# The second expert's output by seven products in two of three token groups instead of one

## The chip, the cores and the metric

The kernel runs on one core of a Trainium2 chip. The metric is the device time of one launch in microseconds (us). Three runs of the kernel before took 972.09, 972.25 and 973.09 us, with a median of 972.25. The engines of the core are TensorE (PE, with its weight loads PEld), VectorE (DVE), ScalarE (ACT), GpSimd (POOL) and SyncE (SP), which issues nearly all DMA transfers here.

## The reference, cut to what matters

```python
attn = block_causal_attention(q, k, v)       # 4 batches x 8 heads, 576 tokens, head size 64
x = attn.reshape(2304, 512)
y = (silu(x @ w_gate) * (x @ w_val)) @ moe_w_out      # first expert, 1536 wide
h = y @ w_in                                          # second expert, 2048 wide
out = where(h > 0, h, exp(min(h, 0)) - 1) @ w_out     # 2304 x 512
```

## The kernel before

**Arithmetic.** Every fp32 product is three matmuls on rounded parts: with a = hi + lo for each operand, hi·hi, lo·hi and hi·lo (`mm3`, L212 to L215, and the output products L1113 to L1115 and L1222 to L1224, which have the same form). "Splitting" an operand means writing its hi with ACT and its lo = operand − hi with DVE or POOL.

**Seven products.** A 2x2 block product needs eight block products. The scheme used here gets by with seven, named M1 to M7, and pays with sums of blocks of both operands before the product (the operands' "sums"), splits of these sums, and adds of the results ("keep" copies a PSUM bank to SBUF, "plus" adds a bank to it). It is used in the gate and value products of some chunks (`sg_unit`, L1374; the sums of its weights lie in the DRAM tile g_scr), for the output of the first expert (`y_group`, L744), for h of the second expert (`p3_h`, L1015) and, in one group of tokens, for its output (`p3_o7`, L1138).

**Stages.** Attention and the first expert's gate stage come first and overlap. Then the tokens run in three groups of 768, each two halves of 384. `y_group` makes y in three groups one after another (466 to 594 us of the profiled execution, the y stage). Then for each group 0, 1 and 2: y is read back and split (`p3_y`, L836; sums L852, hi L860, lo L861), h is made in eight pairs p of 256 columns of W_in (42 matmuls of 384 columns each), the elu is applied and the output product taken. With the constant S7 = 2 (L47), groups 0 and 1 take the plain output product `p3_o` (36 matmuls of 512 columns for each pair, 288 in a group, laid between the h products of the next pair; `p3_drain`, L1121, copies the six banks out). Group 2 takes `p3_o7` behind all its h: 7 products x 8 pairs x 3 blocks of 128 tokens x 3 matmuls = 504 matmuls of 256 columns. Its operand sums are 32 DVE operations (L1149), its 56 splits are an ACT copy (L1157) and a lo (L1158) on POOL where the product is M1 or the pair is 3 or 7, on DVE else; the drains are L1177 (ACT) and L1186 (DVE).

**Weights.** Inputs arrive as 64-bit words; `conv_unit` (L293) loads a block into "raw", DVE makes fp32 of it in a tile c (L196 to L200), ACT writes hi, and DVE or POOL lo. All of W_out ends as the resident parts OH (tiles oh) and OL (ol). The seven-product output needs five kinds of sums or copies of W_out for each pair: `o_sums` (L923) makes them during group 1: it adds OH + OL back to fp32 (L934, 16 DVE operations), takes 32 sums (L940), splits them (hi L950 on ACT, lo L951 on POOL) and stores them in the DRAM tiles o_scr; `o_slot` (L966) loads them from there. The weights of h are loaded from w_scr in the same way, into slots of xa and other tiles.

**Order.** A planner (class Plan, L61 to L147) takes each operation with an engine, a cost, a due time and what it reads and writes, simulates the engines, and writes one fixed program for each engine. Engines then wait for each other only through data and buffers. The loop at the end of the program (L1520 on) hands the steps of the second expert to the planner in the order i, p.

## Time and profile before

| | us |
|---|---|
| median of three runs | 972.25 |
| the profiled execution | 971.81 |
| its span | 970.0 |
| PE busy | 961.0 (99%) |
| DVE busy | 792.4 (82%) |
| ACT busy | 647.0 (67%) |
| POOL busy | 209.3 (22%) |

The profiled execution took 971.81 us, 0.44 us less than the median; 1.81 us of it lie around the span. PE is busy nearly all of the span, so time is won or lost where PE does less or waits. The stages by PE's work are: attention and gate stage up to 466 us, the y stage to 594, group 0 to 732, group 1 to about 846 with the first h of group 2 behind it, and group 2's output by seven products from 904 to 967.

### The profile page before, as it was taken

What the parts mean: (1) busy time and instruction counts of PE and PEld (TensorE: products, weight loads), DVE (VectorE), ACT (ScalarE), POOL (GpSimd) and SP (SyncE); (2) the same over time, 40 slices, a digit from 0 to 9 for tenths busy, and PEclk for the clock granted to TensorE, in tenths of its full rate; (3) what the DMA queues carried; (4) which work ended last, traced back from release to release, by engine and by line L of the source; (5) the groups of instructions that cost most, each with busy time, mean ns of one, the idle gap of its engine ahead of it and who ended that gap; (6) DMA issues with size and microseconds to landing.
All of it is one profiled execution on the core that took longest, in us unless ns stands there. A gap on an engine that the chain in (4) does not pass through costs nothing.

```text
span 970.0 us, 18622 instructions
## 1 busy us (share of the span) xinstructions
PE 961.0 (99%) x6266; PEld 872.7 (90%) x6266; DVE 792.4 (82%) x1637; ACT 647.0 (67%) x1521; POOL 209.3 (22%) x220
## 2 busy tenths in 40 slices
PE   9999999999999999999999999999999999999998
PEld 8789988888888978888999999988899999999998
DVE  6989677767776796699999996989988887868993
ACT  6998578878988644456766675666665555666643
POOL 3334442233315623000000200020001222111231
PEclk9999999999999999999999999999999999999999
DMA  6756465666586669866762802788747676678663
GB/s 226 233 193 219 137 204 163 214 189 218 169 260 209 231 234 336 273 221 199 248 198 88 292 35 83 233 256 303 227 131 217 205 262 206 183 255 256 218 213 115
DMA packets 116463, 202.56 MB, mean 209 GB/s; under 512 B 12304, under 2 KB 51216, under 8 KB 116368
## 3 DMA queue, kind: packets, MB, share of 16 engines
q1 hardware_dynamic: 116224, 201.24, 63.8%
q8 instruction: 50, 0.82, 0.3%
q14 instruction: 45, 0.37, 0.1%
q10 hardware_dynamic: 144, 0.13, 0.0%
HBM read 141.56 MB, written 59.77 MB: 208 GB/s over the span
## 4 chain that ended last, share of the span: by engine, by line
PE 93%; DVE 3%; ACT 2%; issue 1%; DMA 0%; POOL 0%; SPq 0%; ACTq 0%
PE gv L213 7%; PE gv L215 7%; PE gv L214 7%; PE y L213 6%; PE y L214 6%; PE y L215 6%; PE tp L509 5%; PE h L213 5%; PE h L215 5%; PE h L214 5%; PE sa L483 4%; PE o L1115 4%; PE o L1113 4%; PE o L1114 4%; PE tp L604 2%; PE o L1222 2%
## 5 line engine op out<-in xcount | busy, mean ns | idle before, releaser
L213 PE MATMUL gv<-xa,bt 128*128 128x256 f32 x240 | 72.7, 303 | 0.6 <-DVE tt L658 0.6
L213 PE MATMUL gv<-xa,val 128*128 128x256 f32 x240 | 71.9, 300 | 0.0
L609 ACT COPY th<-tp 128x512 f32<-128x512 f32 x96 | 53.5, 590 | 22.1 <-PE tp L605 21.7
L215 PE MATMUL gv<-xa,val 128*128 128x256 f32 x240 | 67.1, 280 | 0.5 <-POOL val L210 0.5
L214 PE MATMUL gv<-xa,bt 128*128 128x256 f32 x240 | 67.0, 279 | 0.0
L215 PE MATMUL gv<-xa,bt 128*128 128x256 f32 x240 | 67.0, 279 | 0.0
L214 PE MATMUL gv<-xa,val 128*128 128x256 f32 x240 | 67.0, 279 | 0.0
L213 PE MATMUL h<-val,xa 128*128 128x384 f32 x194 | 65.2, 336 | 0.0
L215 PE MATMUL h<-val,xa 128*128 128x384 f32 x194 | 65.1, 336 | 0.0
L214 PE MATMUL h<-val,xa 128*128 128x384 f32 x194 | 65.1, 336 | 0.0
L764 ACT ACTIVATE val<-a 128x384 fp32r<-128x384 f32 x80 | 41.3, 525 | 28.3 <-PE y L215 26.6
L1324 POOL TENSOR_TENSOR wy<-c,wy 128x256 fp32r<-128x256 f32 x48 | 39.3, 831 | 88.2 <-ACT wy L1323 88.1
L509 PE MATMUL tp<-th,rv 128*64 128x256 f32 (+1 forms) x512 | 55.5, 359 | 0.0
L918 POOL TENSOR_TENSOR val<-c,val 128x256 fp32r<-128x256 f32 x14 | 12.0, 863 | 196.4 <-ACT val L917 196.4
L918 POOL TENSOR_TENSOR wy<-c,wy 128x256 fp32r<-128x256 f32 x42 | 32.5, 786 | 86.6 <-ACT wy L917 65.6
L951 POOL TENSOR_TENSOR a<-c,a 128x256 fp32r<-128x256 f32 x22 | 19.4, 888 | 146.2 <-ACT a L950 146.2
L653 DVE SCALAR_TENSOR_TENSOR tt<-tt,gv 128x256 f32<-128x256 f32 x60 | 25.0, 416 | 31.4 <-ACT tt L649 31.1
L509 PEld LDWEIGHTS tp<-th,rv 128*64 128x64 f32 x512 | 33.9, 136 | 18.2 <-ACT c L188 0.3
L483 PE MATMUL sa<-rk,rq 64*128 64x320 f32 (+2 forms) x192 | 49.9, 393 | 0.0
L483 PE MATMUL sb<-rk,rq 64*128 64x320 f32 (+2 forms) x192 | 49.9, 393 | 0.0
L213 PEld LDWEIGHTS gv<-xa,bt 128*128 128x128 f32 x240 | 45.3, 189 | 4.8 <-issue 2.6
L213 PEld LDWEIGHTS gv<-xa,val 128*128 128x128 f32 x240 | 45.3, 189 | 2.3 <-issue 2.3
(431 smaller groups left out, 3655.3 us busy)
## 6 DMA issues: line engine op xcount, KB each, us to landing
xa<-w_scr SPq DMA_DIRECT2D x168, 256.0 KB, 3.1
a<-a_scr SPq DMA_DIRECT2D x67, 192.0 KB, 3.4
g_scr<-wy SPq DMA_DIRECT2D x48, 256.0 KB, 2.9
xa<-g_scr SPq DMA_DIRECT2D x48, 256.0 KB, 4.2
w_scr<-wy SPq DMA_DIRECT2D x42, 256.0 KB, 4.0
xa<-o_scr SPq DMA_DIRECT2D x40, 256.0 KB, 3.1
raw<-in_w2i_dram SPq DMA_DIRECT2D x16, 512.0 KB, 4.6
raw<-in_w2o_dram SPq DMA_DIRECT2D x16, 512.0 KB, 4.0
```

The lines of the kernel that those rows point to most:

```text
L213: pe.matmul(dst, wh, xh, start=start, stop=False, skip_group_check=more)
L214: pe.matmul(dst, wh, xl, start=False, stop=False, skip_group_check=more)
L215: pe.matmul(dst, wl, xh, start=False, stop=stop, skip_group_check=more)
L483: pe.matmul(sc[2 * p + j][:, at:at + w], raw["rq"][us, QW * p + 128 * q:QW * p + 128 * q + 128], raw["rk"][us, ext * p + o:ext * p + o + w ...
L509: pe.matmul(st["pv"][64 * j:64 * j + 64, QW * p + o:QW * p + QW], raw["rv"][:, p * (nf + 1) + c, 64 * j:64 * j + 64], x[:, at:at + QW - o] ...
L609: act.copy(out["th", c // 2], st["tr", c])
L764: add("ACT", 412, lambda: act.activation(t(0), ab(p, r, g), ACTF.Copy, scale=0.5), by(u, p), [abk(p, r)], [hk], ([("xcd", o, 0) for o in ( ...
L918: add("POOL", 1000, lambda: pool.tensor_tensor(t()[:, 256:512], part(*x), t()[:, 0:256].bitcast(F32), ALU.subtract), prio, [ck(*x), hk] + ...
L1113: pe.matmul(d, h, OH[f][:, cs], start=(p == 0 and u < 2), stop=False, skip_group_check=True)
L1114: pe.matmul(d, h, OL[f][:, cs], start=False, stop=False, skip_group_check=True)
L1115: pe.matmul(d, l, OH[f][:, cs], start=False, stop=(p == HP - 1 and u > 1), skip_group_check=True)
L1324: add("POOL", 800, lambda: pool.tensor_tensor(t()[:, 256:512], part(*x), t()[:, 0:256].bitcast(F32), ALU.subtract), prio, [ck(*x), hk] + w ...
```

## The change

- S7 is 1: group 1 takes `p3_o7` too, and only group 0 the plain output product.
- The fp32 form of each block of W_out is stored in new DRAM tiles wf_scr once it is converted (`keep_whole`), and `o_sums` loads it from there instead of adding OH + OL; its lo parts go from POOL to DVE. `o_sums` runs for pairs 0 to 4 in group 0 and for 5 and 6 in group 1 (`steps`); pair 7 is converted in the y stage (`early`) and its sums made there (`y_sums`).
- In `y_group` the signs of the weights' sums are turned so that some operand sums become adds in place, and these become DMAs issued by POOL that add the source into the destination (`accum`): one of the two sums before M5 in every group, and both before M6 in group 1 (GA). They take the place of 30 of 72 DVE sums.
- `sg_unit` gives the first two units of the gate stage buffers of their own for the results that are kept, so the planner can lay the products of the two units between each other.
- Buffers move: raw is one tile, one tile of the elu's results lies in it, and four of the six drains of group 0 go to pa_t.

```diff
-S7, HSTEP, OSTEP, OLEAD, PLO, GC, OSL = 2, 7.35, 8.47, 8.0, (3, 7), 1, 6.0
+S7, HSTEP, OSTEP, OLEAD, PLO, GC, OSL = 1, 7.35, 8.47, 8.0, (3, 7), 1, 6.0
+    wf_scr = [dram.tile([128, DM], F32, name=f"wf_scr{f}") for f in range(K2)]
...
+    def keep_whole(f, prio):
+        i = unit["o", f]
+        add("SP", 450, lambda: sp.dma_start(out=wf_scr[f], in_=cv_state[i][1]), prio, [("c", cn[i], 0), ("c", cn[i], 1)], [("wf", f, 0)], data=728)
+
+    def early(f, prio):
+        conv_unit(unit["o", f], prio, whole=True, first=[("w", 2 * K1 - 1 - x, 0) for x in range(3)])
+        keep_whole(f, prio - 1)
...
+        def accum(p, d, x, u):
+            add("POOL", 1000, lambda: pool.dma_start(out=ab(p, d, g), in_=ab(p, x, g), accum_op=ALU.add), by(u, p) - 4, [abk(p, x), abk(p, d)], [abk(p, d)], data=HT * 2.84)
...
             if o == M6:
                 for p in range(KP):
-                    comb(p, 1, 3, 1, ALU.subtract, u)
-                    comb(p, 0, 1, 0, ALU.add, u)
+                    if g != GA:
+                        comb(p, 1, 3, 1, ALU.add, u)
+                        comb(p, 0, 1, 0, ALU.add, u)
+                    else:
+                        accum(p, 1, 3, u)
+                        accum(p, 0, 1, u)
             if o == M5:
                 for p in range(KP):
-                    comb(p, 2, 2, 0, ALU.subtract, u)
-                    comb(p, 0, 3, 0, ALU.subtract, u)
+                    accum(p, 2, 0, u)
+                    comb(p, 0, 0, 3, ALU.subtract, u)
...
+    def o_sums(p, prio, after=[]):
...
+            def load(c=c):
+                full[c] = conv.tile([128, 512], F32, tag="c", name="c", bufs=4)
+                sp.dma_start(out=full[c], in_=wf_scr[2 * p + c])
...
-            add("POOL", 740, lambda: pool.tensor_tensor(t()[:, 256:512].bitcast(F32R), part(*x), t()[:, 0:256], ALU.subtract), prio, [ck(*x), hk], [lk], data=-3000)
+            add("DVE", 420, lambda: dve.tensor_tensor(t()[:, 256:512].bitcast(F32R), part(*x), t()[:, 0:256], ALU.subtract), prio, [ck(*x), hk], [lk], data=-1000)
...
+    seq = "i6 i7 o0 o1 o2 o3 o4 s0 o5 s1 o6 s2 s3 s4 o7".split()
...
-            if i == S7 - 1:
-                o_sums(p, due3[i, p] + OSL)
+            if i == S7 and p == 0:
+                for x in (5,6,):
+                    o_sums(x, due3[i, 0] + 6 * (x - 5) + 2)
```

On PE in the gate stage of seven products, at the first unit's M7 (a bank gv, weights in xa): before, the last product of M7 is followed by M4 into the same bank.

```order
L213 MATMUL gv<-val_132,xa 128x512
L214 MATMUL gv<-val_453,xa 128x512
L215 MATMUL gv<-val_132,xa 128x512
L213 MATMUL gv<-val_132 128x512
L214 MATMUL gv<-val_132 128x512
L215 MATMUL gv<-val_132 128x512
```

The same place after:

```order
L215 MATMUL gv<-val_147,xa 128x512
L216 MATMUL gv<-val_468,xa 128x512
L217 MATMUL gv<-val_147,xa 128x512
L215 MATMUL y_4756<-val_147,xa 128x512
L216 MATMUL y_4756<-val_468,xa 128x512
L217 MATMUL y_4756<-val_147,xa 128x512
L215 MATMUL y_4756<-val_147,xa 128x512
L216 MATMUL y_4756<-val_468,xa 128x512
L217 MATMUL y_4756<-val_147,xa 128x512
L215 MATMUL gv<-val_147 128x512
L216 MATMUL gv<-val_147 128x512
L217 MATMUL gv<-val_147 128x512
```

Six matmuls of the second unit's M7, into a bank y, now stand between the first unit's M7 and its M4.

On POOL from the last weights of the first expert's output into the y stage, before (wy and val hold split weights):

```order
L1324 TENSOR_TENSOR wy_98<-c,wy_98 128x256 x6
L918 TENSOR_TENSOR wy_98<-c,wy_98 128x256 x14
L918 TENSOR_TENSOR val_453<-c,val_453 128x256 x7
L210 TENSOR_TENSOR bt_106<-c,bt_105 128x512
L918 TENSOR_TENSOR val_453<-c,val_453 128x256 x7
```

And after (a and a_N are the operand blocks of the first expert's output):

```order
L982 TENSOR_TENSOR wy_114<-c,wy_114 128x256 x14
L816 DMA a<-a 128x384 x2
L816 DMA a_5974<-a 128x384
L816 DMA a_5975<-a 128x384
L816 DMA a_5976<-a 128x384
L816 DMA a_5977<-a 128x384
L816 DMA a_5984<-a_5978 128x384
L816 DMA a_5985<-a_5979 128x384
L816 DMA a_5986<-a_5980 128x384
L816 DMA a_5987<-a_5981 128x384
L816 DMA a_5988<-a_5982 128x384
L816 DMA a_5989<-a_5983 128x384
```

The first six are the sums before M5 of the first group, the next six the first of two rows of sums before M6 of the second group; six more of the second row (each adds what the first row made) and twelve before M5 of the second and third group follow.

On DVE in the output by seven products, around the sums of M5, before (group 2; L1149 sums, L1158 lo parts, L1186 drains):

```order
L1149 TENSOR_TENSOR a<-a 128x384
L1158 TENSOR_TENSOR bt_122<-g_9615,bt_121 128x384
L1158 TENSOR_TENSOR bt_124<-g_9619,bt_123 128x384
L1186 TENSOR_TENSOR xq_140<-o_7317,xq_140 128x512
L1186 TENSOR_TENSOR xq_140<-o_7318,xq_140 128x256
L1149 TENSOR_TENSOR a<-a 128x384 x2
L1149 TENSOR_TENSOR raw_100<-raw_100,ar_144 128x384
L1158 TENSOR_TENSOR bt_126<-a,bt_125 128x384
```

And after, in group 1, behind the sums of M5 (L1243 lo parts, L1271 drains, L916 and L925 the sums and lo parts of the next group's y):

```order
L1243 TENSOR_TENSOR val_147<-g_8637,val_147 128x384
L916 TENSOR_TENSOR xq_157<-yq_5970,yq_5969 128x768
L925 TENSOR_TENSOR wy_114<-yq_5969,wy_114 128x768
L1243 TENSOR_TENSOR bt_137<-g_8645,bt_136 128x384
L916 TENSOR_TENSOR xq_158<-tt,xq_157 128x768
L1271 TENSOR_TENSOR xq_155<-o_7398,xq_155 128x512
L1271 TENSOR_TENSOR xq_156<-o_7399,xq_156 128x256
L1243 TENSOR_TENSOR bt_139<-tt,bt_138 128x384
L1243 TENSOR_TENSOR bt_141<-a,bt_140 128x384
L1243 TENSOR_TENSOR val_147<-ar_159,val_147 128x384
L925 TENSOR_TENSOR wy_114<-xq_157,wy_114 128x768
```

The sums and splits of y for group 2 (ten operations of 768 columns in all) stand between the lo parts of group 1's seven products; before, they stood beside the plain output products.

## Rows read from the trace of the kernel before

**Rows 1.** The page's chain that ended last, shares of the span by engine.

```profile
PE 93%; DVE 3%; ACT 2%; issue 1%; DMA 0%; POOL 0%; SPq 0%; ACTq 0%
```

**Rows 2.** Windows: PE, PEld, DVE, ACT, POOL busy (instructions), PEclk, DMA share, GB/s.

```profile
466.00:594.00 128.00, 128.00 (x734) 127.45 (x735) 124.79 (x250) 84.63 (x170) 6.48 (x7) 1.00 0.49 158
594.00:732.00 138.00, 137.93 (x702) 125.43 (x701) 116.58 (x215) 86.38 (x183) 6.84 (x8) 1.00 0.70 224
...
856.00:904.00 48.00, 48.00 (x278) 47.91 (x277) 39.84 (x70) 33.55 (x79) 7.27 (x7) 1.00 0.83 258
904.00:967.00 63.00, 62.90 (x525) 62.60 (x523) 48.91 (x89) 31.16 (x67) 18.69 (x13) 1.00 0.56 183
```

**Rows 3.** Timeline of PE: start, duration in us, engine, line, operation, out<-in.

```profile
512.46 0.34 PE L213 MATMUL y<-val,wy 128*128 128x384 f32 x1
...
587.42 0.34 PE L213 MATMUL y<-val,bt 128*128 128x384 f32 x1
...
732.05 0.39 PE L1113 MATMUL o<-xa,val 128*128 128x512 f32 x1
...
856.12 0.40 PE L1115 MATMUL o<-oh,bt 128*128 128x512 f32 x1
...
904.20 0.33 PE L1222 MATMUL o<-xa,val 128*128 128x256 f32 x1
...
966.62 0.28 PE L1224 MATMUL o<-bt,bt 128*128 128x256 f32 x1
```

**Rows 4.** All waits of PE's weight loads from 600 us on: total, count, longest.

```profile
PEld h L213 <- DVE xq L1067: 0.5, 1, 0.5
PEld h L213 <- ACT xq L1071: 0.3, 1, 0.3
```

**Rows 5.** Timeline of PE and SP's queue, start of the seven-product gate stage; brackets: idle before.

```profile
351.76 1.47 SPq L1371 DMA_DIRECT2D xa<-g_scr  x3
...
354.76 0.39 PE L215 MATMUL gv<-xc,bt 128*128 128x512 f32 x1
355.30 0.50 PE L213 MATMUL gv<-xc,bt 128*128 128x512 f32 x1 [0.15 <-DVE tt L658]
...
361.14 0.39 PE L215 MATMUL gv<-val,xa 128*128 128x512 f32 x1
362.21 0.50 PE L213 MATMUL gv<-val 128*128 128x512 f32 x1 [0.68 <-ACT xq L1391]
```

**Rows 6.** Tile g_scr, 330 to 372 us: time from issue to landing of its transfers.

```profile
DMA to landing us min/median/max: 2.0/4.1/6.9
```

**Rows 7.** Timeline of SP's queue and PE in the y stage, second group.

```profile
506.06 3.59 SPq L749 DMA_DIRECT2D a<-a_scr  x4
...
524.96 0.34 PE L213 MATMUL y<-val 128*128 128x384 f32 x1
```

**Rows 8.** Tile a_scr, 480 to 520 us: time from issue to landing of its transfers.

```profile
DMA to landing us min/median/max: 2.3/3.0/3.9
```

**Rows 9.** Timeline of DVE, PE and POOL in group 2's output by seven products.

```profile
913.70 0.55 DVE L1158 TENSOR_TENSOR val<-g,val 128x384 fp32r<-128x384 f32 x1
...
917.15 0.28 PE L1224 MATMUL o<-bt,val 128*128 128x256 f32 x1
...
928.77 2.99 POOL L1158 TENSOR_TENSOR bt<-a,bt 128x384 fp32r<-128x384 f32 x1 [6.73 <-PE o L1224]
...
931.99 0.28 PE L1224 MATMUL o<-xa,bt 128*128 128x256 f32 x1
...
937.78 1.13 POOL L1158 TENSOR_TENSOR val<-g,val 128x384 fp32r<-128x384 f32 x1 [2.50 <-ACT val L1157]
```

**Rows 10.** Groups by line on DVE: count, busy us, mean ns of one, idle before.

```profile
L940 DVE TENSOR_TENSOR c<-c 128x256 f32<-128x256 f32 x32 | 14.1, 447 | 1.5 <-POOL a L951 1.2
L861 DVE TENSOR_TENSOR val<-tt,val 128x768 fp32r<-128x768 f32 x6 | 5.7, 952 | 0.1
```

More of the change, by code (lines that the diff above doesn't have):

```diff
@@ L95, in add @@
         deps.discard(i)
-        self.tasks.append((eng, ns, fn, prio, deps, data, order - deps - {i}, {"POOL": "DVE", "DVE": both and "POOL"}.get(eng), whole))
+        self.tasks.append((eng, ns, fn, prio, deps, data, order - deps - {i}, {"POOL": data <= 0 and "DVE", "DVE": both and "POOL"}.get(eng), whole))
     def order(self):
@@ L776, in keep @@
         def keep(r, m):
-            add("ACT", 450, lambda: act.copy(dst(r, m), bank(X, m)), PMP, [bk(X, m)], [dk(r, m)], free)
+            add("ACT", 450, lambda: act.activation(dst(r, m), bank(X, m), ACTF.Copy, scale=-1.0 if r % 2 else 1.0), PMP, [bk(X, m)], [dk(r, m)], free)
         def plus(r, m, b):
@@ L1515, in attention_moe_moe_kernel, with steps @@
         y_group(g, due2[g])
-    for m, p in W2SEQ[PRE0 + KP:]:
-        if m == "o" and p == 0:
-            add("NONE", 0, to_p3, PT0, writes=[("p3", 0, 0)], behind="p2")
-        if m == "i":
-            p3_weights(p, due3[0, p] - 50, True)
-        else:
-            for f in (2 * p + 1, 2 * p):
-                conv_unit(unit["o", f], due3[0, p] - 20, after=[w2_free(f)])
+    for n, e in enumerate(sorted(EARLY)):
+        early(e, due2[1] + 4 + 4 * n)
+        if e % 2:
+            i = unit["o", e - 1]
+            y_sums(e // 2, due2[1] + 4 + 4 * n + 1, i)
+    add("NONE", 0, to_p3, PT0, writes=[("p3", 0, 0)], behind="p2")
+    def steps(seq):
+        for x in seq:
+            m, p = x[0], int(x[1:])
+            if m == "i":
+                p3_weights(p, due3[0, p] - 50, True)
+            elif m == "s":
+                o_sums(p, due3[0, p] + 20)
+            else:
+                for f in (2 * p + 1, 2 * p):
+                    late(f, due3[0, p] - 20, [w2_free(f)])
+    seq = "i6 i7 o0 o1 o2 o3 o4 s0 o5 s1 o6 s2 s3 s4 o7".split()
+    first = next(n for n, x in enumerate(seq) if x[0] == "s")
+    steps(seq[:first])
     last = None
```

134 lines of the change are left out of this document (96 added, 38 removed).

## The prediction

> **What bounds the kernel now.** I read the chain that ended last first: 93% of it is PE, 3% DVE [rows 1]. The windows by stage come next. From 466 to 967 us PE is busy to within 0.2 us in every stage [rows 2], and from 600 us on its weight loads waited twice, 0.5 and 0.3 us [rows 4]. So there the time is the number of matmuls times their pitch. A single matmul's row shows 0.28 to 0.40 us, but matmuls overlap, and what counts is the distance between starts. With no wait between, two starts and the count of matmuls give it [rows 3]:
> 384 columns, 432 matmuls of the y stage: (587.42 − 512.46) / 432 = 0.1735 us.
> 512 columns: from 732.05 to 856.12 stand all 288 output products of group 1 and 336 of 384 columns, so (124.07 − 336 × 0.1735) / 288 = 0.2284 us.
> 256 columns: from 904.20 to 966.62 stand the 504 of group 2 with 18 h products among them, so (62.42 − 18 × 0.1735) / 503 = 0.1179 us.
>
> The granted clock is 1.00 in all stages [rows 2] and PE stays as busy, so I take that level (2.4 GHz) and these pitches for the new program. What can spoil them is an operand that is late. DVE is the engine to watch: 124.79 of 128 us in the y stage, 116.58 of 138 in group 0, 39.84 of 48 in group 2's h, 48.91 of 63 in its seven products [rows 2]. At 97% in the y stage it still delays nobody, so a high share alone costs nothing; a short lead does.
>
> **Part 1, the swap on PE.** Group 1 loses 288 matmuls of 512 columns and gets 504 of 256: 504 × 0.1179 − 288 × 0.2284 = 59.42 − 65.78 = **−6.4 us**. It lies wholly on the path. Seven products save an eighth of the columns, 12.5%; here 9.7%, because the short matmul costs a little more per column.
>
> **Part 2, the gate stage.** Before, three gaps stand at the start of the seven-product units. The one that the new order can fill: M7's last matmul starts at 361.14, the next at 362.21, with ACT's copy of the bank (L1391) between [rows 5]. At 0.23 us a matmul that is a gap of 0.84. Six matmuls of the second unit, 1.4 us of work, now stand there. Against it the second unit's weights are wanted earlier: their loads are issued at 351.76 and land after a median of 4.1 us [rows 5, 6], at 355.9, and the second unit's first product is now wanted at about 355.0. That is −0.8 to +0.9, and with two smaller gaps (355.30 less 354.76 is 0.54, so 0.31 [rows 5]) −1.5 to +0.9. The planner can lay other products first, so I take **−0.6**.
>
> **Part 3, the accumulating DMAs.** They remove 30 DVE sums and 30 waits of a kind that no row shows: no DMA of the kernel before is issued by POOL. The nearest rows for what one costs POOL are its own operations on 384 columns, 1.13 us alone and 2.99 beside DVE [rows 9]; for the landing, 2.3 to 3.9 us of SP's loads of the same blocks [rows 8]. Call the first c, the second L. The tight place is the second group's two rows of sums before M6. Their last operand is loaded by the last of four transfers issued from 506.06 to 509.65 [rows 7]; issued at about 509.3, it lands 3.0 later, at 512.3. Behind that POOL issues the sixth sum of the first row and six of the second: ready at 512.3 + 7c + L. M6 starts at 524.96 [rows 7] and comes to its third pair of blocks after 24 matmuls, at 529.1; less a hi and a lo of 0.55 each [rows 9] that is 528.0. The spare is 15.7 us. With c = 1.13 and L = 3.0 the chain takes 10.9: hidden. With c = 2 and L = 3.9 it takes 17.9: 2.2 us lost. With c = 2.99 and L = 3.9 it takes 24.8: 9.1 lost. I take **0**, by the 1.13, since POOL has only 6.48 us of other work in that stage [rows 2]. The sums before M5 come two products later and have more room. What the 30 sums free on DVE is used by the conversion of pair 7, which moves into that stage, so DVE is as busy there as before.
>
> The page "SBUF — State Buffer" of the Trainium skill, section "Who interferes with whom", says that DVE's copies and tensor_scalar operations in a two-port mode lock GpSimd out of the port with which it writes descriptors, so that a DMA it issues is starved, while DVE's two-input operations hold only GpSimd's reads. By that the y stage's DVE program, nearly all two-input operations, would leave c near its undisturbed value, and the few conversions of pair 7 would stretch single issues. No trace of before shows a POOL-issued DMA. By the Trainium skill's page "DMA: Bandwidth & Descriptors", section "Anatomy of one DMA — SWDGE (gpsimd) path", 2.0 us and 196.6 KB at 436 KB per us give an estimate of 2.45 us for L; the sum by it would be the same.
>
> **Part 4, group 0.** DVE gets the sums and lo parts for five pairs, 40 operations at 0.447 = 17.9 [rows 10], and loses the conversion of two blocks, which I leave out: at most 116.58 + 17.9 = 134.5 of 138, 97%. The y stage runs at 97% without a wait, so this is hidden; its cover is that these sums are needed only in group 1. SP moves more there: 20 stores of sums, 14 stores and 10 loads of W_out, each 128 x 512 fp32 or 0.26 MB, less two raw blocks of twice that, make 10.5 MB on top of 224 GB/s x 138 us = 30.9 MB. At share 0.70 [rows 2] the 16 DMA engines could carry 44 MB, so the load goes to 94%. Group 2's h ran at 0.83 with PE at 48.00 of 48 [rows 2]. Taken as 0, with up to 3 us against.
>
> **Part 5, group 1.** Its h now looks like group 2's: DVE 39.84 of 48 us, or 9.9 us idle over its 336 x 0.1735 = 58.3. To that come 16 operations on weight sums at 0.447 = 7.2 and the first five operations on group 2's y at 0.952 = 4.8 [rows 10]: 12.0, so DVE enters the seven products about 2.1 us late. There the leads are short: a lo that DVE ended at 914.25 is used at 917.15, 2.9 later, and one that POOL ended at 931.76 (928.77 + 2.99) is used at 931.99, 0.2 later [rows 9]. DVE's delay reaches that POOL operation through the sum it splits, so PE waits about 2.1 − 0.2 = **+1.9**. The other five operations on y (4.8 us) fall where DVE has 14 us idle in 63 [rows 2], behind that place. Bounds: 0 if the planner's order leaves the late work for the idle parts, 6 if all twelve us were late. The o_sums' lo parts that leave POOL cost nothing there.
>
> **The sum.** 971.81 − 6.4 − 0.6 + 1.9 = 966.7 for the profiled execution. This one was 0.44 below the median, so the median is forecast at **967.1 us**.
>
> **The rivals.** I call a difference beyond 0.2% (1.9 us: below 970.3 or above 974.2) faster or slower, about what a measurement of this kernel can tell from no change.
> *A, the forecast*: a stall of 0 to 3 us in group 1 and −1.5 to +0.9 at the gate: 964.3 to 969.7. For it: DVE's 14 idle us in the seven products, and a lead of 2.9 us where it leads least [rows 2, 9].
> *B, DVE bounds group 1 or transfers bound group 0*: stalls of 3 to 5 us in sum where A has 1.9 at its middle: 968.2 to 970.2. For it: DVE would be busy 107 of 118 us in group 1, with POOL's lo parts contending (2.99 against 1.13). Against it: the y stage at 97%.
> *C, the chain of accumulations is late*: c from 2.2 to 2.7 with L = 3.9 loses 3.6 to 7.1 us: 970.7 to 974.2, no change. For it: two landings in a row on the same block. Against it: an idle POOL.
> *D, the accumulations are starved*: c = 2.99 and L = 3.9, 9.1 us lost, 976.2: slower. The point is 7c + L above 22.8. For it: POOL's operation beside a busy DVE did take 2.99, and DVE is busiest just there. The page's rule on locked ports stands against most of it.
> *E, better than forecast*: no stall, the gate's gaps gone: 971.81 + 0.44 − 6.4 − 1.5 = 964.3 or less.
>
> **How the numbers follow.** A 0.55, E 0.05, B 0.18, C 0.12, D 0.10. Faster: A, E and B, 0.78; same: C, 0.12; slower: D, 0.10. The likeliest is A: 967.1. The range leaves out D and the upper half of C (0.16), and little below: 963.0 to 972.0.
>
> **What would show it.** PE back to back at 0.118 us through group 1's 504 products, about 59 us long, proves part 1; a PE wait there on a lo part of DVE or POOL proves and sizes part 5. A wait of PE on a split in the second group's M6, with POOL's issue as the step before it, is C or D; POOL's DMA rows give c directly. DVE's share in group 0 should be between 90 and 97%. A wait on weights in group 0 would be the transfers. The forecast is wrong if M6 of the second y group waits more than 3 us, or if PE waits in group 1 sum to more than 4.

## The result, and the profile after

The changed kernel took 978.77 us (median of 8 runs, 974.52 to 987.94) against 972.73 us of the kernel before (8 runs): a ratio of 1.0085, with a 95% interval of 1.0064 to 1.0105. It is slower, by 0.62% as the medians stand and by 0.85% as the ratio has it, to which the longer runs add, where 0.5% faster was forecast. The ratios here leave out one slow run in all, of e11_o7first, 1057.21 us at a mean granted clock of 0.85. The profiled execution took 978.47 us with a span of 976.4, 6.4 us more than the span before. Its page gives the engines so (busy us, share of the span, instructions), and its chain that ended last, against [rows 1], has PE at 80% instead of 93%, with DVE, DMA, ACT and POOL in its place:

```profile
PE 957.5 (98%) x6482; PEld 875.6 (90%) x6482; DVE 797.7 (82%) x1664; ACT 654.9 (67%) x1550; POOL 246.8 (25%) x238
...
PE 80%; DVE 6%; DMA 6%; ACT 3%; POOL 2%; issue 2%; SPq 1%; ACTq 0%; DVEq 0%; POOLq 0%
```

PE has less to do, 957.5 us instead of 961.0, and waits more. From 300 us on PE itself waited before only at the end of the gate stage, 2.2 us in all (total us, times, longest):

```profile
PE gv L213 <- ACT xq L1391: 0.8, 2, 0.7
PE y L213 <- ACT xq L1391: 0.7, 1, 0.7
PE gv L213 <- DVE tt L658: 0.7, 2, 0.6
```

After the change there are thirteen such rows that sum to 11.4 us; the seven largest:

```profile
PE o L1309 <- POOL val L1243: 2.2, 1, 2.2
PE h L215 <- DMA xa<-w_scr: 1.6, 2, 0.9
PE o L1198 <- DVE bt L212: 1.2, 1, 1.2
PE o L1309 <- POOL bt L1243: 1.1, 1, 1.1
PE y L215 <- ACT xq L1478: 1.0, 1, 1.0
PE y L216 <- DVE xa L825: 0.8, 3, 0.5
PE y L215 <- ACT val L824: 0.8, 1, 0.8
```

They name four releasers, POOL, DVE, ACT and the DMA engines; the row of L1478 is at the end of the gate stage, where before stood one of 0.7, and the others are spread over four stages. The 9.2 us of waits more are about the 3.5 us of work less and the 6.4 us of span more. No single wait holds the 6.4 us. The windows by stage, in the columns of [rows 2] (y stage, group 0, group 1's h, its seven products, group 2's h, its seven products):

```profile
466.00:594.00 128.00, 125.60 (x707) 122.23 (x706) 118.28 (x238) 83.43 (x177) 40.47 (x41) 1.00 0.87 246
594.00:732.00 138.00, 136.02 (x691) 122.98 (x690) 120.63 (x242) 88.12 (x192) 3.83 (x4) 1.00 0.82 276
732.00:791.00 59.00, 56.76 (x317) 54.42 (x316) 50.31 (x98) 41.08 (x96) 7.57 (x7) 1.00 0.91 315
791.00:857.00 66.00, 62.70 (x525) 62.30 (x525) 56.43 (x95) 34.60 (x70) 29.61 (x13) 1.00 0.66 204
857.00:911.00 54.00, 54.00 (x313) 53.90 (x312) 41.70 (x75) 36.55 (x85) 7.18 (x7) 1.00 0.79 247
911.00:974.00 63.00, 62.14 (x526) 61.62 (x524) 50.43 (x91) 32.32 (x69) 17.57 (x13) 1.00 0.60 186
```

The first four stages wait, the last two hardly. The DMA share went from 0.49 to 0.87 in the y stage and from 0.70 to 0.82 in group 0, and it is 0.91 in group 1's h.

To compare kernels I cut each trace at four PE instructions that all have: A, the last 256-column gate product that waits for DVE (349.41 us before); B, the first 512-column product of the second expert (608.80); C, the 288th, the last of group 0 (731.82); D, PE's last (966.62). "Gate and y" is A to B, "group 0" B to C, "groups 1, 2" C to D. From one profile each, in us:

| kernel | gate and y | group 0 | groups 1, 2 |
|---|---|---|---|
| before | 259.4 | 123.0 | 234.8 |
| changed | 263.0 | 125.9 | 234.2 |
| difference | +3.6 | +2.8 | −0.6 |

These three and a start later by 0.45 make the +6.3 of PE's end. The forecast was −0.6, 0 and −6.4 + 1.9 = −4.5.

### The profile page after: what moved, and what is told of

Same layout as the page of the kernel before. It is cut to its first block, busy times and chain, and to the rows that moved or that the text cites. A ratio compares the mean times of both kernels' runs of the same rounds, so it can differ in the third digit from the quotient of the medians.

```text
span 976.4 us, 19357 instructions
## 1 busy us (share of the span) xinstructions
PE 957.5 (98%) x6482; PEld 875.6 (90%) x6482; DVE 797.7 (82%) x1664; ACT 654.9 (67%) x1550; POOL 246.8 (25%) x238
## 4 chain that ended last, share of the span: by engine, by line
PE 80%; DVE 6%; DMA 6%; ACT 3%; POOL 2%; issue 2%; SPq 1%; ACTq 0%; DVEq 0%; POOLq 0%
PE gv L215 8%; PE gv L217 7%; PE gv L216 7%; PE tp L543 5%; PE sa L517 4%; PE y L216 4%; PE y L217 4%; PE y L215 4%; PE o L1309 4%; PE o L1307 3%; PE o L1308 3%; PE h L215 3%; PE h L217 3%; PE h L216 3%; PE tp L638 2%
## 5 line engine op out<-in xcount | busy, mean ns | idle before, releaser
L216 PE MATMUL gv<-xa,bt 128*128 128x256 f32 x240 | 67.0, 279 | 0.0
L216 PE MATMUL gv<-xa,val 128*128 128x256 f32 x240 | 66.9, 279 | 0.0
L816 POOL DMA_DIRECT2D a<-a x30 | 26.4, 982 | 122.9 <-DVE xq L813 89.7
L824 ACT ACTIVATE val<-a 128x384 fp32r<-128x384 f32 x80 | 40.2, 522 | 19.0 <-PE y L217 15.0
L215 PE MATMUL h<-val,xa 128*128 128x384 f32 x148 | 50.0, 338 | 1.1 <-DMA xa<-w_scr 0.9
L217 PE MATMUL h<-val,xa 128*128 128x384 f32 x148 | 49.7, 336 | 0.0
L216 PE MATMUL h<-val,xa 128*128 128x384 f32 x148 | 49.7, 336 | 0.0
L190 ACT ACTIVATE c<-raw 128x512 f32<-128x512 f32 x60 | 40.1, 679 | 13.3 <-DMA raw<-in_w2o_dram 6.1
```

Source lines behind the costliest of these rows:

```text
L190: act.activation(c, raw.bitcast(I32)[:, 1::2].bitcast(F32), ACTF.Abs, scale=float(2.0 ** -112))
L215: pe.matmul(dst, wh, xh, start=start, stop=False, skip_group_check=more)
L216: pe.matmul(dst, wh, xl, start=False, stop=False, skip_group_check=more)
L217: pe.matmul(dst, wl, xh, start=False, stop=stop, skip_group_check=more)
L824: add("ACT", 412, lambda: act.activation(t(0), ab(p, r, g), ACTF.Copy, scale=0.5), by(u, p), [abk(p, r)], [hk], ([("xcd", o, 0) for o in ( ...
```

## The experiments

Unless a diff says otherwise each starts from the changed kernel. Ratios are to the kernel before, from the same chip, with 95% intervals.

**The gate stage alone**, in the kernel before:

```diff
-        hc = lambda n: ys_b[n % 4]
+        hc = lambda n: tt_b[2] if n is None else ys_b[n % 4]
...
+        m1, u2, u3 = ((hcn[0], hcn[1], hcn[3]), (None, hcn[2], hcn[4]))[f] if f < 2 else (nxt("hc") for _ in range(3))
```

> The kernel before with one part of the change alone: the first two units of the gate stage of seven products get buffers of their own, so that their products are interleaved on PE. Theory: the three gaps of 0.31, 0.31 and 0.84 us at 354 to 362 us close and the second unit's weights come in time, so the y stage starts 1.0 to 1.5 us earlier, and since from there PE is back to back, the whole time falls by that: about 971.4. Rival (the second unit's weights land late, or DVE falls behind by its shifted adds): 0 to +0.9.

Measured: 972.64 us, ratio 1.0002 (0.9993 to 1.0011). The waits of [rows 5] are gone, but the one at the stage's end grew from 0.7 to 1.0 us and small ones came in the y stage; gate and y took 259.35 us, as before. The expected 1.0 to 1.5 us did not come: this part is worth nothing that can be measured.

**The accumulating DMAs, and the early pair.** Four kernels, with the changed one or e3_plo (below) as the fourth corner.

```diff
-            add("POOL", 1000, lambda: pool.dma_start(out=ab(p, d, g), in_=ab(p, x, g), accum_op=ALU.add), ...)
+            comb(p, d, d, x, ALU.add, u)
```

> The changed kernel with all 30 accumulating DMAs of the y stage put back as DVE sums of 128x384; all else as changed. In the changed kernel the y stage loses 5.1 us to PE waits. Theory (the accumulating transfers land late, 7.5 us at the median, and keep the DMA engines busy): those waits go, the time falls by 4 to 5 us, to about 974. Rival (what was moved into the stage with pair 7, its conversion and sums, fills DVE and blocks ACT): DVE gets 30 x 0.47 = 14 us more on top of 118.3 of 128, so its share passes 100%, the waits stay or grow, and the time is the same or up to 5 us more.

```diff
-    EARLY = {2 * p + x for p in (7,) for x in range(2)}
+    EARLY = set()
...
-                for x in (5,6,):
+                for x in (5, 6, 7):
```

> The changed kernel without the early pair: pair 7 of W_out converted with the others in group 0, its sums made in group 1 behind those of 5 and 6. Accumulating DMAs stay. Theory (the accumulating transfers cost the y stage its 5.1 us): the y stage still loses 3 us or more, and group 1's h gets 16 more operations on DVE, so the time is the same or up to 3 us more. Rival (pair 7's work costs the y stage): the y stage runs without waits, the time falls by 4 to 5 us there, less what group 1 then loses.

> e4_noearly (pair 7 of W_out converted in group 0 and its sums made in group 1, accumulating DMAs kept) with the lo parts of pairs 3 and 7 in group 1 on DVE as in e3_plo. With the next run it fills the table of early pair and accumulating DMAs. Theory (the early pair is what costs the y stage; the accumulating DMAs alone cost it nothing): from the gate stage's first 256-column product to the first output product of the second expert 258.5 to 259.5 us, as before the change (259.4). Rival (transfers at 0.8 of the DMA engines' time, of which the accumulating ones take a third, cost it by themselves): 261 us or more.

> e14_noearly_plo with the 30 accumulating DMAs put back as DVE sums: the y stage then holds what it held before the change. Theory: 259 to 260 us for the same stretch, so that the accumulating DMAs save or cost less than 1 us where the early pair is not there, and are needed only to make room for it. Rival (something else of the change costs the y stage, such as the turned signs, the order or the gate stage): 261 us or more here too.

| gate and y, us | 30 accumulating DMAs | 30 DVE sums |
|---|---|---|
| early pair | 263.0 (changed), 260.7 (e3_plo) | 266.5 (e1_noacc) |
| no early pair | 258.7 (e4_noearly), 259.3 (e14) | 260.3 (e15) |

The whole times were 992.73 us for e1_noacc (ratio 1.0205, 1.0142 to 1.0267), 984.51 for e4_noearly (1.0128, 1.0079 to 1.0178), 980.03 for e14 (1.0081, 1.0055 to 1.0108) and 988.35 for e15 (1.0148, 1.0128 to 1.0167). So the rival of e1_noacc holds: without the accumulating DMAs the early pair costs the stage more, not less. The pair costs 4.3, 1.4 and 6.2 us in the three matched pairs of the table. Each is from one profile, and one profile tells this stretch to some 3 us only: nine kernels that give DVE, ACT and POOL the very same program in it (the changed one, e3_plo and seven below) took 260.7 to 266.2 us, 262.4 in the mean, against 259.4 before the change. So the sign is shown and the size is not. Without the pair PE waits 0.2 us there in all (e4_noearly, L216 for DVE's lo part of L825).

The accumulating DMAs cost the stage no time that the table shows, but they are most of the load on its DMA engines. The stage with the pair alone (e1_noacc), with neither (e15) and with the accumulating DMAs alone (e4_noearly), in the columns of [rows 2], where the share before was 0.49:

```profile
466.00:594.00 128.00, 126.57 (x716) 123.94 (x717) 124.18 (x258) 81.39 (x173) 8.16 (x5) 1.00 0.52 170
466.00:594.00 128.00, 127.25 (x724) 125.12 (x723) 125.96 (x257) 81.38 (x171) 10.42 (x8) 1.00 0.54 173
466.00:594.00 128.00, 127.79 (x733) 126.93 (x732) 119.98 (x236) 85.97 (x180) 40.54 (x43) 1.00 0.80 225
```

But the pair's conversion then stands in group 0, which can't take it: PE waits 5 us (e4, e14) and 11 us (e15) for ACT's hi of the last pair (L208).

What late landings do to the stage is seen in the changed kernel's ACT and DVE at 490 us (start, duration, engine, line; brackets: idle before, and what ended it):

```profile
489.63 0.66 ACT L190 ACTIVATE c<-raw 128x512 f32<-128x512 f32 x1 [4.24 <-DMA raw<-in_w2i_dram]
490.19 0.51 ACT L824 ACTIVATE val<-a 128x384 fp32r<-128x384 f32 x1
...
490.73 0.56 DVE L825 SCALAR_TENSOR_TENSOR val<-a,val 128x384 fp32r<-128x384 f32 x1 [2.42 <-ACT val L824]
...
490.75 0.44 PE L215 MATMUL y<-val,val 128*128 128x384 f32 x1 [0.76 <-ACT val L824]
```

ACT stands 4.24 us before a conversion whose raw block hasn't landed; the split behind it in its program (L824) is ready to go and isn't reached; DVE's lo waits for that and PE for both. DVE was not too busy, it idled. The DMA engines' share was 0.93 from 480 to 500 us, 0.67 before. That block is one of W_in, converted in this stage before the change too, and the stall is there without the pair: 2.16 us in e4_noearly, where PE doesn't wait, and 3.3 in e14. The kernels without accumulating DMAs don't have it. So it belongs to the load on the DMA engines, and how the pair makes it cost PE time is argued, not shown.

What is seen with the pair and not without it is the second group's M2, for which the last three blocks land late (in the changed kernel):

```profile
514.23 1.62 SPq L806 DMA_DIRECT2D a<-a_scr  x3
DMA to landing us min/median/max: 7.7/9.3/10.2
...
524.08 0.52 ACT L824 ACTIVATE xa<-a 128x384 fp32r<-128x384 f32 x1 [1.59 <-DMA a<-a_scr]
...
526.19 0.44 PE L215 MATMUL y<-xa,val 128*128 128x384 f32 x1 [0.32 <-ACT xa L824]
```

In e4_noearly the same three are issued 4 us earlier and land sooner:

```profile
DMA to landing us min/median/max: 4.8/5.3/6.0
```

From start to start of PE's products the changed kernel loses 1.7 us at 490 us and 1.9 at M2.

The accumulating DMAs themselves, from the same trace (their time on POOL in ns, minimum, median, maximum; then KB each and the median us from issue to landing, beside SP's loads of the same blocks):

```profile
L816 POOL DMA_DIRECT2D a<-a x30: 859/874/1524, 480.1 to 572.2; - x30
a<-a_scr SPq DMA_DIRECT2D x59, 192.0 KB, 4.5
a<-a POOLq DMA_DIRECT2D x30, 192.0 KB, 7.5
```

**The second y group's sums on DVE**, from e3_plo:

```diff
-GA, CD, WO0, XO, AC, UG, GW0, GWS, WOL = 1, 5, ...
+GA, CD, WO0, XO, AC, UG, GW0, GWS, WOL = 9, 5, ...
```

> e3_plo with the sums before M6 in the second y group on DVE (12 operations, 5.6 us) instead of 12 of the 30 accumulating DMAs. Theory (the accumulating DMAs relieve DVE and cost little; what the y stage loses comes from pair 7's conversion): DVE, at 94% of the stage, goes to 98%, and the y stage loses 1 to 3 us more than e3_plo's 1.4. Rival (the wait at 524 us is the chain of the accumulates before M6, ready too late): that wait goes, and the time falls by about 1 us.

Measured: 980.60 us, 1.0087 (1.0071 to 1.0102), gate and y 266.5: the theory's sign; the median is 4.9 us above e3_plo's. The rival's wait at 524 us did go and the time didn't fall. With the early pair in the stage DVE needs these twelve accumulating DMAs.

**The early pair later.** The run starts from e5_poollo (below) and not from e3_plo: the lo parts of W_out's sums are back on POOL in it as well.

```diff
-            add("DVE", 420, lambda: dve.tensor_tensor(t()[:, 256:512].bitcast(F32R), ...
+            add("POOL", 740, lambda: pool.tensor_tensor(t()[:, 256:512].bitcast(F32R), ...
...
-        early(e, due2[1] + 4 + 4 * n)
+        early(e, due2[1] + 24 + 4 * n)
...
-            y_sums(e // 2, due2[1] + 4 + 4 * n + 1, i)
+            y_sums(e // 2, due2[1] + 24 + 4 * n + 1, i)
```

> e3_plo with the early pair 7 due 20 us later in the y stage, where the DMA engines are less busy (0.5 to 0.1 in the last 20 us). Theory (the y stage loses 3 to 5 us because ACT, in order, waits for raw blocks that land late at 0.99 to 1.1 of the DMA engines' time): the waits at 490 and 524 us shrink, the stage loses 1 to 2 us, the time is 1 to 2 us below e3_plo. Rival (it is DVE's load, the same wherever the pair is put): the loss moves to the third group of the stage and keeps its size.

Measured: 981.32 us, 1.0090 (1.0072 to 1.0108). The later due time moved nothing: DVE, ACT, POOL and SP run e5_poollo's program, operation for operation, and gate and y (261.8 us, 261.9 in e5_poollo) and group 0 (130.3, 131.2) are those of e5_poollo. So this run says nothing on a later place for the pair, which stays untested; it is a second measurement of e5_poollo.

**POOL's lo parts in group 1.**

```diff
-            eng, en, ns = (pool, "POOL", 1100) if u == 0 or p in PLO else (dve, "DVE", 557)
+            eng, en, ns = (pool, "POOL", 1100) if u == 0 or i > S7 and p in PLO else (dve, "DVE", 557)
```

> The changed kernel with the lo parts of pairs 3 and 7 in group 1's output by seven products on DVE instead of POOL (12 operations; M1's stay on POOL, group 2 unchanged). Theory (POOL's lo stretches to 7.6 and 9.0 us while DVE runs two-input operations without a pause): both PE waits of 1.1 and 2.2 us go, and DVE, with 9.6 us idle in the 66 of that stage, takes the 12 x 0.47 = 5.6 us: 2 to 3.5 us faster, about 975.5. Rival (DVE is late there anyway, and the wait is for the sum before the lo): the waits turn into waits for DVE of the same or more size, and the time is the same or up to 2 us more.

Measured: 975.72 us, 1.0024 (1.0012 to 1.0036), 3 us less than the changed kernel. All that PE waits for behind 791 us is one load:

```profile
PE o L1307 <- DMA xa<-o_scr: 0.8, 1, 0.8
```

So group 1's seven products run here without a stop, and their pitch can be read: 504 products with 42 products of the next h between them stand from the first to the last of

```profile
790.44 0.28 PE L1307 MATMUL o<-xa,val 128*128 128x256 f32 x1
856.98 0.28 PE L1309 MATMUL o<-bt,bt 128*128 128x256 f32 x1
```

With 0.1735 us for each h product that is 0.1178 us each, where the forecast took 0.1179.

In the changed kernel POOL's operations on 128x384 are, in group 1 at M3 and M5, and in group 2 at the slowest:

```profile
820.24 7.64 POOL L1243 TENSOR_TENSOR bt<-a,bt 128x384 fp32r<-128x384 f32 x1 [3.29 <-ACT bt L1242]
...
833.66 8.98 POOL L1243 TENSOR_TENSOR val<-g,val 128x384 fp32r<-128x384 f32 x1 [3.07 <-ACT val L1242]
...
936.44 3.00 POOL L1243 TENSOR_TENSOR bt<-a,bt 128x384 fp32r<-128x384 f32 x1 [6.74 <-ACT bt L1242]
```

The first ends at 827.88, 0.87 us after DVE, which had run sums and splits without a gap, stopped for 1.7 us; the second ends at 842.64, 0.87 us after DVE's next pause began, one of 0.17 us:

```profile
826.07 0.94 DVE L916 TENSOR_TENSOR xq<-tt,xq 128x768 f32<-128x768 f32 x1
828.71 1.02 DVE L1271 TENSOR_TENSOR xq<-o,xq 128x512 f32<-128x512 f32 x2 [1.70 <-PE o L1309]
...
841.94 1.11 DVE L1243 TENSOR_TENSOR bt<-a,bt 128x384 fp32r<-128x384 f32 x1 [0.17 <-ACT bt L1242]
```

The sums and splits of the next group's y (L916, L925) are what fills DVE's gaps there; group 2 has none of them behind it, and POOL's longest is 3.0, as in [rows 9].

**The same, the other way round**: POOL's lo parts stay, y's work moves.

```diff
-        p3_y(i, due3[i, 0] - 20)
+        p3_y(i, due3[i, 0] - (60 if i == 2 else 20))
```

> The changed kernel with POOL's lo parts kept, and the ten sums and lo parts of group 2's y on DVE moved 40 us forward, from beside M3 and M5 to the beginning of group 1's output by seven products (M1 and M2). Theory (POOL's lo parts of pairs 3 and 7 stretch to 7.6 and 9.0 us where DVE runs two-input operations from SBUF without a pause): at M3 and M5 DVE has pauses again, POOL's operations there last 1 to 4 us, and the PE waits on them (1.1 and 2.2 us) go; 2 to 3 us below the changed kernel, unless M2's lo parts now wait. Rival (POOL's long operations come with M3 and M5 themselves, as the group's sums do): they stay at 6 us and more, and so do the waits.

Measured: 983.65 us, 1.0122 (1.0093 to 1.0151). POOL's operations at M3 and M5 fell to 3 us, as the theory said:

```profile
822.34 2.98 POOL L1243 TENSOR_TENSOR bt<-a,bt 128x384 fp32r<-128x384 f32 x1 [7.08 <-ACT bt L1242]
...
839.25 2.95 POOL L1243 TENSOR_TENSOR val<-g,val 128x384 fp32r<-128x384 f32 x1 [3.05 <-ACT val L1242]
```

and PE now waited for a lo part of DVE at M2, behind the ten operations put there:

```profile
PE o L1309 <- DVE val L1243: 5.4, 1, 5.4
```

Both runs together show the cause: beside the ten operations that DVE has for the next y, POOL's lo parts are late, and behind them DVE's own are.

**The plain product in group 1** (S7 = 2 with all else as changed; group 1's output then reads blocks of W_out that the staging of the sums has overwritten, with the same instructions):

```diff
-S7, HSTEP, ... = 1, 7.35, ...
+S7, HSTEP, ... = 2, 7.35, ...
```

> The changed kernel with S7 = 2: the plain output product in group 1 again, all else as changed. Theory: the swap itself is worth 6.4 us on PE less the 3.6 us that PE waits for two lo parts of POOL in group 1's seven products, so this kernel is about 3 us slower than the changed one, about 981; loss in the y stage and in group 0 stays. Rival (the swap pays nothing or costs, since the weight loads of the second seven-product group also cause the 2.4 us of waits for w_scr): the same time as the changed kernel or up to 3 us less.

Measured: 977.63 us, 1.0063 (1.0042 to 1.0084), 1.1 us below the changed kernel's median, with intervals that overlap: not the theory's 3 us slower, and within the rival's range. Everything around the swap costs 5 us by itself; the swap then gives nothing in the changed kernel (978.77), and some 2 us once POOL's waits are gone (975.72).

**W_out's sums.** First those of pairs 5 and 6, from e3_plo moved, then left out, then all left out:

```diff
-    seq = "i6 i7 o0 o1 o2 o3 o4 s0 o5 s1 o6 s2 s3 s4 o7".split()
+    seq = "i6 i7 o0 o1 o2 o3 o4 s0 o5 s1 o6 s2 s3 s4 o7 s5 s6".split()
...
-                for x in (5,6,):
+                for x in ():
```

> e3_plo with the sums of W_out's pairs 5 and 6 made at the end of group 0's program instead of during group 1's h (8 stores, 4 loads of 0.26 MB and 16 DVE operations moved). Theory (in group 1's h the DMA engines are 91 to 93% busy with 18.6 MB in 59 us, and the 4 us of PE waits there are loads of w_scr that land late): 3.1 MB less in that window, the share falls to some 80% as in group 2's h, and these waits fall to 1 us or less; group 0 may lose part of it again: 1 to 3 us below e3_plo. Rival (the loads are late because their slots come free late, or because of DVE): the waits on w_scr stay as they are.

Measured: 978.21 us, 1.0059 (1.0035 to 1.0083), from 974.82 to 982.69: not faster than e3_plo. In its profile, of the fastest run, the waits on w_scr went from 2.2 to 1.7 us only, and the share in 732 to 761 us was 0.95 (0.94 in e3_plo), since the moved transfers ran over into it. This run doesn't tell the two theories apart; the next tells more.

```diff
-                for x in (5,6,):
+                for x in ():
...
-            sp.dma_start(out=ws[n].bitcast(F32).rearrange("p h f -> p (h f)"), in_=o_scr[p][OST.index(o)])
+            sp.dma_start(out=ws[n].bitcast(F32).rearrange("p h f -> p (h f)"), in_=o_scr[p % 5][OST.index(o)])
```

> e3_plo without the sums of W_out's pairs 5 and 6 (left out: 16 DVE operations on sums, 8 stores and 4 loads of 0.26 MB during group 1's h; the output of pairs 5 to 7 then uses the sums of pairs 0 to 2, with as many loads). Theory (in group 1's h the loads of w_scr, 0.26 MB for each 1.04 us of PE, land late because other transfers share the DMA engines): with 3.1 MB less of 18.6 in 59 us the DMA share at 732 to 791 us falls from 0.93 to about 0.8, the PE waits on w_scr fall from 2.2 us to 0.5 or less, the time by about 2 us against e3_plo, to 973.5. Rival (slots of the weights come free late, whatever else is moved): w_scr waits of 2 us stay, and the time is that of e3_plo.

Measured: 973.17 us, 1.0004 (0.9988 to 1.0020), 2.5 us below e3_plo, about as expected. PE's waits at 732 to 791 us, and the landing of the loads of w_scr, in e3_plo:

```profile
PE h L215 <- DVE g L1128: 1.1, 1, 1.1
PE h L215 <- DMA xa<-w_scr: 1.1, 2, 0.9
PE o L215 <- DMA xa<-w_scr: 1.1, 2, 0.8
...
DMA to landing us min/median/max: 2.7/5.0/7.5
```

and in e10_no56, with its window:

```profile
PE h L215 <- DMA xa<-w_scr: 0.4, 1, 0.4
...
DMA to landing us min/median/max: 2.8/3.9/7.7
...
732.00:791.00 59.00, 58.16 (x336) 56.70 (x335) 48.59 (x88) 41.24 (x93) 7.19 (x7) 1.00 0.86 280
```

The share fell from 0.93 to 0.86 (about 0.8 was expected), the landing by 1.1 us, the waits on w_scr from 2.2 us to 0.4, and the one of 1.1 us on DVE went. The edit takes out 16 operations of DVE as well as the transfers, so the run doesn't split the two. Before the change the same loads landed in 3.1 us, at a share of 0.70. The plain output products stood between the h products then: a pair took 15.5 us of PE for seven loads of 0.26 MB, and without them 7.3. That faster rate alone makes no wait: group 2's h had it already and ran without one, at a share of 0.83 before and 0.79 after, with landings of 3.3 and 3.4 us. What group 1's h has besides are the transfers for the sums and for the next y.

```diff
-    seq = "i6 i7 o0 o1 o2 o3 o4 s0 o5 s1 o6 s2 s3 s4 o7".split()
+    seq = "i6 i7 o0 o1 o2 o3 o4 o5 o6 o7".split()
...
-                for x in (5,6,):
+                for x in ():
...
-            sp.dma_start(out=ws[n].bitcast(F32).rearrange("p h f -> p (h f)"), in_=o_scr[p][OST.index(o)])
+            sp.dma_start(out=ws[n].bitcast(F32).rearrange("p h f -> p (h f)"), in_=o_scr[p if o == M1 else 7][OST.index(o)])
```

> e3_plo without the sums of W_out's pairs 0 to 6 (left out: 56 DVE operations on sums and lo parts, 28 stores and 14 loads of 0.26 MB in groups 0 and 1; the output by seven products uses the sums of pair 7 for all pairs, with as many loads). Theory (group 0 loses its 2 us and group 1's h its 4 us to the making of these sums, by DVE's load and by transfers): the waits in both go, 2 us less than e10_no56, so the whole is some 971 us, and of the 6.4 us of PE work saved 3 or more are seen behind the y stage's loss of 1.4 to 3. Rival (the loads of w_scr and o_scr in group 1 and the conversions in group 0 are late by themselves): no change against e10_no56, 973.2.

Measured: 970.47 us, 0.9971 (0.9958 to 0.9984): faster than before, though gate and y still lost time in its profile, of the longest of its runs (266.2). Group 0 took 123.5 us and groups 1, 2 230.1: 4.7 less than before the change, with these waits left from 594 us on:

```profile
PE o L215 <- DMA xa<-w_scr: 0.4, 1, 0.4
PE h L215 <- DMA xa<-w_scr: 0.4, 1, 0.4
PE h L215 <- ACT xq L1155: 0.2, 1, 0.2
```

The gain of the swap is there; making its weights in the time at hand eats it. Here too operations of DVE and transfers go together, so which of the two eats more is open.

**Shedding DVE, or changing the order.** The lo parts of the sums back on POOL, from e3_plo:

```diff
-            add("DVE", 420, lambda: dve.tensor_tensor(t()[:, 256:512].bitcast(F32R), ...
+            add("POOL", 740, lambda: pool.tensor_tensor(t()[:, 256:512].bitcast(F32R), ...
```

> The changed kernel with the lo parts of pairs 3 and 7 in group 1 on DVE (as e3_plo), and the lo parts of W_out's sums of pairs 0 to 6 back on POOL (28 operations of 128x256). Theory (group 0 loses its 2 to 3 us because DVE, 87% busy there and with conversions in its order, is late): DVE sheds 20 x 0.42 = 8.4 us in group 0 and 3.4 in group 1, the waits at 720 to 745 us go, and the time is 1.5 to 3 us below e3_plo, about 973.5. Rival (the waits come from transfers that land late, to which ACT and DVE are held in order): the same time as e3_plo, within 1 us; or more, where POOL stretches beside DVE and holds the buffers of the sums.

Measured: 982.23 us, 1.0095 (1.0081 to 1.0108), group 0 131.2 us instead of e3_plo's 125.0: the planner's new order put pair 7's conversion and the splits of the h results late. The theory failed.

Pair 7's conversion ahead of three sums, from e3_plo without the early pair:

```diff
-    seq = "... s0 o5 s1 o6 s2 s3 s4 o7".split()
+    seq = "... o5 s0 o6 s1 o7 s2 s3 s4".split()
```

> e3_plo without the early pair, with pair 7 of W_out converted ahead of the sums of pairs 2 to 4 instead of behind them, and its sums made in group 1. Theory (pair 7's work in the y stage costs 2 to 4 us there; the 5 us wait of e4_noearly at 717 us was the late place of pair 7's conversion in group 0): the y stage runs as before the change, the wait at 717 us goes, group 1's h pays 1 to 2 us more for 8 stores and loads: 974 to 976, the same as e3_plo or 1.5 us below. Rival (group 0 is full, with any order some conversion is late): a wait of 3 us or more stays in group 0, and the time is 978 or more.

Measured: 978.63 us, 1.0071 (1.0045 to 1.0097). Its profile ran at a mean clock of 0.95, so its stretches are compared with care. The time is the rival's, the place isn't: PE has no wait from 612 to 734 us, and group 0 took 118.3 us. Gate and y, without the early pair, took 262.2 us at that clock, as long as with the pair in other kernels: one more reason not to read the pair's size from one profile. Waits of 1.5, 0.7 and 2.6 us stand at 734 to 742 us, where group 1's h begins, on splits of DVE and ACT. The work left group 0 and was late behind it.

Last, a planner that expects transfers later, from the y stage on, by 2.0 and by 3.5 us:

```diff
-    MARG, ALONE, WAITH, CVP = 0.0, ...
+    MARG, ALONE, WAITH, CVP = 2000.0, ...
```

> e3_plo with a margin in the planner from the y stage on: it takes ACT and DVE to see a transfer 2.0 us later than before, so it puts other work ahead of an operation that waits for one. The computation is the same. Theory (ACT, in the order that it was given, stands still for transfers that land later than planned, and splits and adds wait behind it): PE's waits on ACT and DVE splits in the y stage and in group 0 shrink, 1 to 2 us below e3_plo, 974. Rival (the transfers are late as a whole and what waits for them is needed by then; the order can't help): the same as e3_plo or slower, with waits of the same sum in other places.

> As e17_marg2000 with a margin of 3.5 us. Theory: of the same size or better by up to 1 us where the landings are 4 to 8 us late; a version that is below 972.7 would beat the kernel before. Rival: the margin pushes conversions of W_out and sums so late that group 0 or group 1 waits for them, 978 or more.

Measured: 991.09 us (1.0190, 1.0169 to 1.0211) and 992.79 us (1.0221, 1.0182 to 1.0260). Gate and y took 262.1 and 263.3 us, groups 1, 2 230.9 and 231.8, but group 0 141.2 and 141.8, with one wait:

```profile
PE o L1197 <- ACT bt L208: 12.1, 1, 12.1
```

The rival held: what the margin put aside was the conversion of W_out's last pair, and that is needed at the end of group 0. ACT came to it late, behind splits of W_out's sums for which it stood 1.4 to 2.7 us each, waiting for stores to free their slots and for DVE. No version with the swap that computes the reference beat the kernel before; e3_plo came nearest, 0.24% slower.

## Why the prediction was wrong

**What bounds the kernel, and part 1, the swap on PE: right.** Group 1's swap was put at −6.4 us. Without W_out's sums (e16_nosums) groups 1 and 2 fell by 4.7 us with 1.0 us of waits left; 0.7 stays open. In e3_plo the products of group 1 ran at 0.1178 us each, where 0.1179 was taken. The matmuls were priced well; the failure is in what has to feed them.

**Part 2, the gate stage: mis-sized.** −0.6 us was taken; e8_gate measured 0.0 (±0.9). The gaps closed and the time didn't fall, so closing a gap in a row isn't yet a gain in the stage.

**Part 3, the accumulating DMAs: the bounds on c and L were both off, and the result stood in part by luck.** c was bounded by POOL's own operations, 1.13 to 2.99; it was 0.87 at the median. L was bounded by SP's loads of the same blocks, 2.3 to 3.9; it was 7.5 at the median and 12.5 for the last sum before M6. The estimate of 2.45 us that the prediction gave beside its sum was off further; the measurement decides. 7c + L is 13.6 with the medians, below the spare of 15.7, and the table of four shows no loss by it. But POOL also stood still for 4.9 us between the two rows of sums, since the second row had to wait for DVE's lo parts, and the last sum landed at 529.27, 1.3 us after the 528.0 by which the forecast had M6 need it. ACT waited for it for 0.8 us and PE didn't, because M2 ahead of it was late and M6 began at 528.30 instead of 524.96. In e11_o7first, without the early pair, PE waited 0.5 us there. So rival C's chain came close; D's danger didn't show. What the part left out is the other half of the price: the accumulating DMAs load the DMA engines (from 0.54 to 0.80 of the stage, e15 to e4_noearly), and the plain loads beside them land later. The page "SBUF — State Buffer" of the Trainium skill, "Who interferes with whom", infers that DVE's operations with two inputs don't hold the port with which GpSimd writes descriptors. The trace agrees, at most 1.52 us each beside a DVE that was busy 92% of the stage.

**The step that failed first: pair 7 at nothing.** "What the 30 sums free on DVE is used by the conversion of pair 7 … so DVE is as busy there as before" counted one engine's busy time. DVE was in fact less busy than before (118.3 of 128 us against 124.8). The DMA share went from 0.49 to 0.87, most of it by the accumulating DMAs, and landings got late: a raw block of W_in took 8.27 us at 490 us, M2's last blocks 7.7 to 10.2. ACT, in order, stood before them, once with a split ready behind, and PE waited. Gate and y was forecast at −0.6 and came out at +3.6 in the changed kernel, +3.0 in the mean of the nine. By the table the pair cost 1.4 to 4.3 us beside the accumulating DMAs, where nothing was forecast; that it costs is shown, how it turns the load into PE's waits only in M2.

**Part 4, group 0: taken as 0, up to 3 us against; it was +2.8** (+2.0 in e3_plo, +0.5 without the sums). The direction of the bound was right. DVE's and the DMA engines' shares were forecast at 97% and 94% and came out lower, 87% and 82%, and PE waited all the same: a share that leaves room isn't a cover for work that has to be done in order by a certain time.

**Part 5, group 1: the right place, half of the size, and a mechanism left out.** 1.9 us of stall were forecast for the lo parts of DVE and POOL. POOL's took 3.6 us of PE from start to start, and not because DVE was late: POOL's operation itself went from 1 to 9 us beside an unbroken DVE. The row 2.99 beside 1.13 stood in [rows 9], and I used it for the price of a DMA issue and not for the twelve operations of the very same kind that the change puts beside ten more DVE operations. The page "SBUF — State Buffer" of the Trainium skill, "Who interferes with whom", also says that a DVE operation with two SBUF inputs does contend with a GpSimd instruction that reads SBUF; the traces agree: 7.64 and 8.98 us beside them, 2.98 and 2.95 when the y work was moved away. That it lasts over a whole row of DVE's operations, until DVE pauses, is what these traces show. And "its h now looks like group 2's" was followed for DVE only. The DMA share of group 2's h, 0.83, stood in [rows 2] too, and there PE had no wait; with the sums and the y loads on top it became 0.91 in group 1's, loads of w_scr landed after 4.7 us instead of 3.1, and PE waited 2.1 us for them. The transfers were counted in group 0, not here.

**The rivals.** The outcome is B's kind, late DVE work and transfers in groups 0 and 1, with the y stage and POOL's held operations added; B was held to 3 to 5 us in sum because the parts were priced one by one and the changed kernel has all of them. D's sign came for another reason than D's.

## What to carry to other kernels

When work moves into a stage, price it on every shared resource there, the DMA engines and the in-order queues of each engine as much as the busy shares: a load that lands late costs what stands behind it in that engine's program, even on an engine with time to spare. Where PE's filler work is taken out of a stage, the weight loads of what is left come faster; compute bytes per us of PE for the stage as it will be, with the transfers that other work adds there. If a trace shows an operation stretched by a neighbour, use that row for every operation of its kind that gets the neighbour, and not only for the new ones.

## What the runs showed of the hardware that was not expected

A POOL operation on 128x384, 1.0 us alone, took up to 11.66 us in e1_noacc, beside DVE operations in a row. PE then waited 6.4 us, and the granted clock fell behind the wait (same columns as [rows 2]):

```profile
840.00:850.00 10.00, 9.91 (x85) 9.70 (x83) 10.00 (x17) 5.79 (x11) 5.41 (x1) 1.00 0.80 251
850.00:860.00 10.00, 3.69 (x17) 3.70 (x18) 5.96 (x10) 2.64 (x6) 7.73 (x3) 0.66 0.24 68
860.00:870.00 10.00, 10.00 (x87) 10.00 (x86) 5.39 (x10) 4.08 (x8) 2.52 (x3) 1.00 0.77 208
```

At 0.66 the mean lies between the two levels of 1.2 and 2.4 GHz, in the stretch with PE's wait. It was below 1.00 around the waits of 5 us and more too, in e4_noearly (0.66), e14 (0.66) and e15 (0.58). Around shorter waits both were seen: 1.00 around 2.2 us in the changed kernel, 0.83 around 1.9 us in e14 (780 to 790 us) and 0.93 around 2.5 us in e13_ga (550 to 560). The changed kernel's runs spread over 13 us, with mean clocks from 1.0 down to 0.993 in the longest; e3_plo's, without these POOL operations, over 3.5 us. That POOL's operation runs from 6 to 12 us by chance in the long runs fits this, but no profile of such a run was taken, so it stays open. An accumulating DMA between two SBUF tiles costs POOL 0.87 us at the median (0.98 in the mean), about as much as POOL's own operation on such a block (1.0), and lands after 7.5 us, up to 12.5.
